# A gated recurrence and a two-layer tanh-shrink network on one core: a shorter polynomial, no elementwise work on GpSimd, the mask on ScalarE, and contiguous token slots

## The chip, the cores and the metric

The kernel runs on one core of a Trainium2 chip. The metric is the device time of one execution in microseconds (us). Engine names in the profile: PE is TensorE's matmul side, PEld its weight loads, DVE is VectorE, ACT is ScalarE, POOL is GpSimd, SP issues the transfers. "L262" is line 262 of the kernel that the profile belongs to; lines move by a few between kernels. "Records" are matmuls as the profile lists them: it has two records for each float32 matmul of the two layers and one for each transpose. "STT" in the prediction is a scalar_tensor_tensor operation of DVE, which takes two tensors and a scalar.

## The reference

```python
# x, f_logit: (4, 6080, 256) float32; lower_bound: (256,)
f = lower_bound + (1 - lower_bound) * sigmoid(f_logit)
h = 0
for t in range(S):                    # along the sequence, for each channel
    h = f[:, t] * h + (1 - f[:, t]) * x[:, t]
    y[:, t] = h
# moe_w_in: (256, 2048), moe_w_out: (2048, 256), float64
h = y.reshape(B * S, D) @ w_in        # 24320 tokens
g = h - tanh(h)
out = g @ w_out
```

The difference `h - tanh(h)` loses its digits where h is small, so both kernels compute it a second way, with a polynomial in h squared, and choose element by element.

## The kernel before

Tokens go through in 47 blocks of 512 and one of 256. A block has 8 slots. In each slot TensorE computes two chunks of 128 rows of h (4 matmuls of 512 columns, 8 records, hT) and, for the block before, 8 matmuls of the second layer (256 columns, 16 records, psO). Between these, four slots carry the pieces of the next block's recurrence (transposes, sigmoid, f, v, scan). The first block also turns the eight weight pieces from float64 bits into float32 on DVE.

The elementwise part of a slot, on tiles of 128 partitions by 1024:

```python
nc.scalar.copy(out=hs, in_=hT[:, :, 0:nb])
nc.scalar.activation(out=t, in_=hT[:, :, 0:nb], func=AF.Square)
nc.scalar.activation(out=th, in_=hT[:, :, 0:nb], func=AF.Tanh)
for n, (a, _, _) in enumerate(QUADS):                      # two quadratics in t
    nc.scalar.activation(out=sq[n], in_=t, func=AF.Square, scale=a, bias=...)
nc.vector.tensor_scalar(out=mask, in0=t, scalar1=SMALL, scalar2=None, op0=ALU.is_lt)
nc.gpsimd.tensor_tensor(out=g, in0=hs, in1=th, op=ALU.subtract)
nc.gpsimd.tensor_tensor(out=hs, in0=hs, in1=t, op=ALU.mult)
for n, (_, _, c) in enumerate(QUADS):
    nc.vector.scalar_tensor_tensor(out=hs, in0=sq[n], scalar=c, in1=hs, op0=ALU.add, op1=ALU.mult)
nc.vector.copy_predicated(out=g, mask=mask, data=hs)
```

The second layer reads its weights (the stationary operand) from g with a step of `ns` = 4 tokens, and inputs and outputs lie in memory so that one partition holds four tokens in a row:

```python
lhsT=gs[j, fc // 2][:, fc % 2, i:nb:ns]                    # second_layer
in_=srcs[s][t0 : t0 + nb, :].rearrange("(p i) d -> p i d", p=P)   # fetch
```

The next block but one is fetched at the end of a block: a store and two loads stand behind each other in one queue.

## Time and profile before

| | before |
|---|---|
| median (lowest to highest; a fourth run came later, with the result) | 3606.25 us (3606.09 to 3609.78, 3 runs) |
| span of the profiled execution | 3607.2 us |
| one block, store to store | 73.3 us |
| busy: DVE, TensorE, ACT, GpSimd | 96%, 84%, 55%, 61% of the span |

The shares are quoted in the prediction, with the rows of the operations. Two more views belong to the argument. The first is the chain of work that ended last, by engine, as the page of the kernel before has it: the shares say on which engine the end depended for how long.

```profile
DVE 60%; issue 24%; ACT 8%; POOL 4%; PE 3%; DMA 1%; DVEq 0%; SPq 0%; ACTq 0%; POOLq 0%
```

The second is the table of waits of the kernel before: engine, tile and line, whom it waited for, us in all, times, the longest.

```profile
ACT hs L249 <- DVE gT L265: 1439.8, 353, 10.6
...
PE tT L173 <- DMA fn<-in_f_logit_dram: 250.3, 46, 6.6
```

ACT, far from busy, is held back by DVE in nearly every slot. TensorE's longest wait comes once a block, for the transfer of f_logit, while DVE goes on working: that wait cost nothing.

### The profile page before, as it was taken

How to read it: one execution, taken by the hardware profiler on the slowest of the kernel's cores; microseconds unless marked ns; L12 is line 12 of the kernel's file. 1: busy time of each engine (PE TensorE's matmuls, PEld its weight loads, DVE VectorE, ACT ScalarE, POOL GpSimd, SP SyncE). 2: the span in 40 equal slices, each digit the busy share in tenths (PEclk: the TensorE clock that was granted, in tenths of full speed). 3: DMA queues.
4: the chain of work that ended last, by engine and by line, in shares of the span. 5: the costliest groups of instructions: out<-in, count | busy, mean ns of one | idle time of the engine just before them, and what ended most of it. 6: DMA issues, size and time to landing. Idle time of an engine off the chain costs nothing.

```text
span 3607.2 us, 27433 instructions
## 1 busy us (share of the span) xinstructions
PE 3021.7 (84%) x9912; PEld 2187.5 (61%) x9912; DVE 3448.1 (96%) x1898; ACT 1970.7 (55%) x2207; POOL 2186.1 (61%) x774
## 2 busy tenths in 40 slices
PE   2388888888888888888888888888888888888888
PEld 1166656666666656666666656665666666665667
DVE  6699999999999999999999999999999999999996
ACT  2255555555555555555555555555555555555554
POOL 2256666666666666666666666666666666666664
PEclk7699999999999989999999999999999999999999
DMA  2100000000100010000000010001000000001000
GB/s 93 35 18 18 18 30 23 18 18 18 35 18 18 18 35 18 18 18 25 28 18 18 18 35 18 18 18 35 18 18 18 21 32 18 18 18 35 18 12 15
DMA packets 24344, 84.87 MB, mean 24 GB/s; under 512 B 2704, under 2 KB 2704, under 8 KB 24208
## 3 DMA queue, kind: packets, MB, share of 16 engines
q1 hardware_dynamic: 24208, 83.11, 6.7%
q8 instruction: 79, 1.29, 0.2%
q14 instruction: 57, 0.47, 0.0%
HBM read 58.20 MB, written 24.90 MB: 23 GB/s over the span
## 4 chain that ended last, share of the span: by engine, by line
DVE 60%; issue 24%; ACT 8%; POOL 4%; PE 3%; DMA 1%; DVEq 0%; SPq 0%; ACTq 0%; POOLq 0%
DVE hs L262 25%; DVE gT L265 16%; DVE mask L256 10%; DVE f L197 6%; ACT s L253 2%; ACT hs L249 2%; POOL hs L260 2%; ACT t L250 2%; POOL gT L259 2%; DVE v L201 2%; PE psO L281 2%; PE hT L234 1%; ACT th L251 1%; DVE y L213 1%; DMA fn<-in_f_logit_dram 0%
## 5 line engine op out<-in xcount | busy, mean ns | idle before, releaser
L259 POOL TENSOR_TENSOR gT<-hs,th 128x1024 f32<-128x1024 f32 (+1 forms) x384 | 967.8, 2520 | 1373.9 <-ACT th L251 1263.5
L234 PE MATMUL hT<-y,w_in 128*128 128x512 f32 (+1 forms) x3072 | 1532.4, 647 | 197.0 <-DVE w_in L148 105.4
L281 PEld LDWEIGHTS psO<-w_out,gT 128*128 128x128 f32 x6080 | 1474.3, 326 | 160.7 <-issue 87.6
L281 PE MATMUL psO<-w_out,gT 128*128 128x256 f32 x6080 | 1476.5, 396 | 24.8 <-DVE w_out L148 15.3
L249 ACT COPY hs<-hT 128x1024 f32<-128x1024 f32 (+1 forms) x384 | 385.4, 1004 | 1611.8 <-DVE gT L265 1439.8
L260 POOL TENSOR_TENSOR hs<-hs,t 128x1024 f32<-128x1024 f32 (+1 forms) x384 | 1217.6, 3171 | 30.1
L262 DVE SCALAR_TENSOR_TENSOR hs<-s,hs 128x1024 f32<-128x1024 f32 (+1 forms) x768 | 1131.0, 1473 | 78.6 <-POOL hs L260 37.1
L234 PEld LDWEIGHTS hT<-y,w_in 128*128 128x128 f32 x3072 | 634.1, 214 | 858.0 <-issue 736.3
L265 DVE COPY_PREDICATED gT<-mask,hs 128x1024 f32<-128x1024 uint8 (+1 forms) x384 | 1081.8, 2817 | 20.3 <-PE hT L234 0.5
L253 ACT ACTIVATE s<-t,shift 128x1024 f32<-128x1024 f32 (+1 forms) x768 | 836.6, 1150 | 0.0
L256 DVE TENSOR_SCALAR mask<-t 128x1024 uint8<-128x1024 f32 (+1 forms) x384 | 640.0, 1667 | 33.9 <-ACT t L250 33.9
L251 ACT ACTIVATE th<-hT 128x1024 f32<-128x1024 f32 (+1 forms) x384 | 393.1, 1024 | 0.0
L250 ACT ACTIVATE t<-hT 128x1024 f32<-128x1024 f32 (+1 forms) x384 | 392.4, 1022 | 0.0
L213 DVE TENSOR_TENSOR_SCAN y<-f,y,v 128x512 f32<-128x512 f32 (+4 forms) x94 | 297.0, 3160 | 3.4
L173 PE MATMUL tT<-ident,fn 128*128 128x128 f32 x380 | 79.2, 345 | 250.3 <-DMA fn<-in_f_logit_dram 250.3
L197 DVE TENSOR_SCALAR f<-u,nom 128x512 f32<-128x512 f32 (+1 forms) x96 | 238.0, 2480 | 0.1
L173 PEld LDWEIGHTS tT<-ident,fn 128*128 128x128 f32 x380 | 57.3, 177 | 268.3 <-DMA fn<-in_f_logit_dram 259.4
L173 PE MATMUL tT<-ident,xn 128*128 128x128 f32 x380 | 67.9, 307 | 110.1 <-DVE v L201 108.9
L173 PEld LDWEIGHTS tT<-ident,xn 128*128 128x128 f32 x380 | 49.7, 157 | 129.0 <-DVE v L201 122.3
L289 ACT COPY osb<-psO 128x256 f32<-128x256 f32 x190 | 71.9, 378 | 15.9 <-PE psO L281 15.9
L201 DVE SCALAR_TENSOR_TENSOR v<-u,om,tT 128x512 f32<-128x512 f32 (+1 forms) x96 | 70.0, 729 | 0.0
L185 ACT ACTIVATE u<-tT 128x512 f32<-128x512 f32 (+1 forms) x96 | 57.5, 599 | 5.1 <-PE tT L173 5.1
(21 smaller groups left out, 81.3 us busy)
## 6 DMA issues: line engine op xcount, KB each, us to landing
fn<-in_f_logit_dram SPq DMA_DIRECT2D x47, 512.0 KB, 4.1
xn<-in_x_dram SPq DMA_DIRECT2D x47, 512.0 KB, 5.1
out_dram<-osb SPq DMA_DIRECT2D x47, 512.0 KB, 2.9
raw<-in_moe_w_in_dram SPq DMA_DIRECT2D x4, 1024.0 KB, 6.5
raw<-in_moe_w_out_dram SPq DMA_DIRECT2D x4, 1024.0 KB, 5.1
fn<-in_f_logit_dram SPq DMA_DIRECT2D x1, 256.0 KB, 3.2
xn<-in_x_dram SPq DMA_DIRECT2D x1, 256.0 KB, 3.4
out_dram<-osb SPq DMA_DIRECT2D x1, 256.0 KB, 2.0
```

What stands on the lines that cost most here:

```text
L197: nc.vector.tensor_scalar(out=f[:, 0:nb], in0=u[:, 0:nb], scalar1=nom[:, h : h + 1], scalar2=1.0, op0=ALU.mult, op1=ALU.add,)
L234: nc.tensor.matmul(hT[:, c, 0:nb], lhsT=w_in_cols(2 * p + c, k), rhs=ys[j][:, k, 0:nb], start=(k == 0), stop=(k == KC - 1),)
L249: nc.scalar.copy(out=hs, in_=hT[:, :, 0:nb])
L250: nc.scalar.activation(out=t, in_=hT[:, :, 0:nb], func=AF.Square)
L251: nc.scalar.activation(out=th, in_=hT[:, :, 0:nb], func=AF.Tanh)
L253: nc.scalar.activation(out=sq[n], in_=t, func=AF.Square, scale=a, bias=shift[:, n : n + 1])
L256: nc.vector.tensor_scalar(out=mask, in0=t, scalar1=SMALL, scalar2=None, op0=ALU.is_lt)
L259: nc.gpsimd.tensor_tensor(out=g, in0=hs, in1=th, op=ALU.subtract)
L260: nc.gpsimd.tensor_tensor(out=hs, in0=hs, in1=t, op=ALU.mult)
L262: nc.vector.scalar_tensor_tensor(out=hs, in0=sq[n], scalar=c, in1=hs, op0=ALU.add, op1=ALU.mult)
L265: nc.vector.copy_predicated(out=g, mask=mask, data=hs)
L281: nc.tensor.matmul(ps[:], lhsT=gs[j, fc // 2][:, fc % 2, i:nb:ns], rhs=w_out_rows(fc), start=(fc == 0), stop=(fc == FC - 1),)
```

## The change

The intent is to take GpSimd out of the way of DVE, to shorten the elementwise work, and to speed up the weight loads. Where h squared is below 0.16 the value is tanh(h) times h squared times one quadratic in h squared. The slot then has four passes on ACT and four on DVE, none on GpSimd; the subtraction reads h straight from PSUM; the predicated copy of one slot is issued in the middle of the next. Besides, f_logit and x are transposed together into one PSUM tile, that pool has three tiles, and all weight loads are issued at the start. The scratch tiles have three buffers instead of two. The core of the diff (cut; deleted comments, renamed tiles, buffer counts in SBUF and the joined transposes are left out):

```diff
-SMALL = 0.35
-QUADS = (...)
+SMALL = 0.16
+QA, QB, QC = -0.045459185935280914, 0.24438677692776334, 0.2736084102289697
 ...
-    ps_t = ctx.enter_context(tc.tile_pool(name="ps_t", bufs=2, space=PSUM))
-    ps_h = ctx.enter_context(tc.tile_pool(name="ps_h", bufs=2, space=PSUM))
+    ps_h = ctx.enter_context(tc.tile_pool(name="ps_h", bufs=3, space=PSUM))
 ...
-                in_=srcs[s][t0 : t0 + nb, :].rearrange("(p i) d -> p i d", p=P),
+                in_=srcs[s][t0 : t0 + nb, :].rearrange("(i p) d -> p i d", p=P),
 ...
+        nc.scalar.activation(out=t, in_=h, func=AF.Square)
+        nc.scalar.activation(out=th, in_=h, func=AF.Tanh)
+        nc.scalar.activation(out=sq, in_=t, func=AF.Square, scale=QA, bias=bias[:, 0:1])
+        nc.scalar.activation(
+            out=small, in_=t, func=AF.Relu, scale=-1.0, bias=bias[:, 1:2]
+        )
+        nc.vector.tensor_tensor(out=g, in0=h, in1=th, op=ALU.subtract)
+        nc.vector.scalar_tensor_tensor(
+            out=sq, in0=sq, scalar=QC, in1=th, op0=ALU.add, op1=ALU.mult
+        )
+        choose()
+        nc.vector.tensor_tensor(out=sq, in0=sq, in1=t, op=ALU.mult)
+        late.append((g, small.bitcast(INT32), sq))
+
+    def choose():
+        if late:
+            g, mask, q = late.pop()
+            nc.vector.copy_predicated(out=g, mask=mask, data=q)
 ...
-                lhsT=gs[j, fc // 2][:, fc % 2, i:nb:ns],
+                lhsT=gs[j, fc // 4][:, fc % 4, i * P : (i + 1) * P],
 ...
-        for n in order[:3]:
+        for n in order:
             fetch_weight(n)
```

More of the change, by code (lines that the diff above doesn't have):

```diff
@@ L15 @@
 P = 128
-SMALL = 0.35
-QUADS = (
-    (0.2820323407649994, 0.18348582088947296, 0.5017573237419128),
-    (0.2820323407649994, -0.6548143625259399, 0.1937771886587143),
-)
+SMALL = 0.16
+QA, QB, QC = -0.045459185935280914, 0.24438677692776334, 0.2736084102289697
 @with_exitstack
@@ L69 @@
     const = ctx.enter_context(tc.tile_pool(name="const", bufs=1))
-    rawpool = ctx.enter_context(tc.tile_pool(name="raw", bufs=3))
     natpool = ctx.enter_context(tc.tile_pool(name="nat", bufs=2))
@@ L73 @@
     ypool = ctx.enter_context(tc.tile_pool(name="ypool", bufs=2))
-    tpool = ctx.enter_context(tc.tile_pool(name="tpool", bufs=2))
-    gpool = ctx.enter_context(tc.tile_pool(name="gpool", bufs=2 * NP))
+    tpool = ctx.enter_context(tc.tile_pool(name="tpool", bufs=3))
+    gpool = ctx.enter_context(tc.tile_pool(name="gpool", bufs=NP))
     opool = ctx.enter_context(tc.tile_pool(name="opool", bufs=2))
-    ps_t = ctx.enter_context(tc.tile_pool(name="ps_t", bufs=2, space=PSUM))
-    ps_h = ctx.enter_context(tc.tile_pool(name="ps_h", bufs=2, space=PSUM))
+    ps_h = ctx.enter_context(tc.tile_pool(name="ps_h", bufs=3, space=PSUM))
     ps_o = ctx.enter_context(tc.tile_pool(name="ps_o", bufs=2, space=PSUM))
@@ L84 @@
     nom = const.tile([P, KC], FP32, name="nom")
-    shift = const.tile([P, 2], FP32, name="shift")
+    bias = const.tile([P, 2], FP32, name="bias")
     w_in = [const.tile([P, KC * TB], FP32, name=f"w_in{g}") for g in range(NG)]
@@ L101, in fetch_weight @@
         g = n % NG
-        raw = rawpool.tile([P, KC * TB], mybir.dt.int64, name="raw")
+        raw = gpool.tile([P, KC * TB], mybir.dt.int64, name="raw", tag="gT")
         if n < NG:
@@ L119, in round_weight @@
         dst = weights[n][:]
-        e = tpool.tile([P, KC * TB], INT32, name="e", tag="hs")
+        e = tpool.tile([P, KC * TB], INT32, name="e", tag="sq")
         m = tpool.tile([P, KC * TB], INT32, name="m", tag="t")
@@ L166 @@
     us = {}
-    def turn(j, s, h):
-        ns = sizes[j] // P
-        dst = ps_t.tile([P, NQ, P], FP32, name="tT")
-        for i in range(ns):
-            nc.tensor.transpose(
-                dst[:, i, :], nats[j, s][:, i, h * P : (h + 1) * P], ident[:]
-            )
-        return dst[:, 0:ns, :].rearrange("p i m -> p m i")
-    def by_slot(t, nb):
-        return t[:, 0:nb].rearrange("p (m i) -> p m i", m=P)
     def gate(j, h):
         nb = sizes[j]
-        fT = turn(j, 0, h)
+        both = ps_h.tile([P, 2, TB], FP32, name="fx", tag="hT")
+        for s in range(2):
+            for i in range(nb // P):
+                nc.tensor.transpose(
+                    both[:, s, i * P : (i + 1) * P],
+                    nats[j, s][:, i, h * P : (h + 1) * P],
+                    ident[:],
+                )
         u = midpool.tile([P, TB], FP32, name="u")
-        nc.scalar.activation(out=by_slot(u, nb), in_=fT, func=AF.Sigmoid, scale=-1.0)
-        us[j, h] = u
+        nc.scalar.activation(
+            out=u[:, 0:nb], in_=both[:, 0, 0:nb], func=AF.Sigmoid, scale=-1.0
+        )
+        us[j, h] = (u, both)
     def recur(j, h):
@@ L192, in recur @@
             ys[j] = ypool.tile([P, KC, TB], FP32, name="y")
-        y, u = ys[j], us.pop((j, h))
-        xT = turn(j, 1, h)
+        y = ys[j]
+        u, both = us.pop((j, h))
         f = midpool.tile([P, TB], FP32, name="f")
         v = midpool.tile([P, TB], FP32, name="v")
+        nc.vector.scalar_tensor_tensor(
+            out=v[:, 0:nb], in0=u[:, 0:nb], scalar=om[:, h : h + 1],
+            in1=both[:, 1, 0:nb], op0=ALU.mult, op1=ALU.mult,
+        )
         nc.vector.tensor_scalar(
@@ L199, in recur @@
             op0=ALU.mult, op1=ALU.add,
-        )
-        nc.vector.scalar_tensor_tensor(
-            out=by_slot(v, nb), in0=by_slot(u, nb), scalar=om[:, h : h + 1], in1=xT,
-            op0=ALU.mult, op1=ALU.mult,
         )
@@ L224 @@
     gs = {}
+    late = []
     def first_layer(j, p):
         nb = sizes[j]
-        hT = ps_h.tile([P, 2, TB], FP32, name="hT")
+        hT = ps_h.tile([P, 2, TB], FP32, name="hT", tag="hT")
         for c in range(2):
@@ L240, in first_layer @@
                 )
-        def temp(tag, dtype=FP32):
-            return tpool.tile([P, 2, TB], dtype, name=tag, tag=tag)[:, :, 0:nb]
-        hs, t, th, mask = temp("hs"), temp("t"), temp("th"), temp("mask", UINT8)
-        sq = [temp("s0"), temp("s1")]
-        gT = gpool.tile([P, 2, TB], FP32, name="gT")
-        g = gT[:, :, 0:nb]
-        nc.scalar.copy(out=hs, in_=hT[:, :, 0:nb])
-        nc.scalar.activation(out=t, in_=hT[:, :, 0:nb], func=AF.Square)
-        nc.scalar.activation(out=th, in_=hT[:, :, 0:nb], func=AF.Tanh)
@@ L252, in first_layer @@
-        for n, (a, _, _) in enumerate(QUADS):
-            nc.scalar.activation(
-                out=sq[n], in_=t, func=AF.Square, scale=a, bias=shift[:, n : n + 1]
-            )
-        nc.vector.tensor_scalar(
-            out=mask, in0=t, scalar1=SMALL, scalar2=None, op0=ALU.is_lt
-        )
-        nc.gpsimd.tensor_tensor(out=g, in0=hs, in1=th, op=ALU.subtract)
-        nc.gpsimd.tensor_tensor(out=hs, in0=hs, in1=t, op=ALU.mult)
-        for n, (_, _, c) in enumerate(QUADS):
-            nc.vector.scalar_tensor_tensor(
-                out=hs, in0=sq[n], scalar=c, in1=hs, op0=ALU.add, op1=ALU.mult
-            )
@@ L265, in first_layer, with temp @@
-        nc.vector.copy_predicated(out=g, mask=mask, data=hs)
-        gs[j, p] = gT
+        h = hT[:, :, 0:nb]
+        def temp(tag):
+            return tpool.tile([P, 2, TB], FP32, name=tag, tag=tag)[:, :, 0:nb]
+        t, th, sq, small = temp("t"), temp("th"), temp("sq"), temp("small")
+        if p % 2 == 0:
+            gs[j, p // 2] = gpool.tile([P, 4, TB], FP32, name="gT", tag="gT")
+        c0 = 2 * (p % 2)
+        g = gs[j, p // 2][:, c0 : c0 + 2, 0:nb]
+        nc.scalar.activation(out=t, in_=h, func=AF.Square)
@@ new lines, in first_layer @@
+        nc.scalar.activation(out=th, in_=h, func=AF.Tanh)
+        nc.scalar.activation(out=sq, in_=t, func=AF.Square, scale=QA, bias=bias[:, 0:1])
+        nc.scalar.activation(
+            out=small, in_=t, func=AF.Relu, scale=-1.0, bias=bias[:, 1:2]
+        )
+        nc.vector.tensor_tensor(out=g, in0=h, in1=th, op=ALU.subtract)
+        nc.vector.scalar_tensor_tensor(
+            out=sq, in0=sq, scalar=QC, in1=th, op0=ALU.add, op1=ALU.mult
+        )
+        choose()
+        nc.vector.tensor_tensor(out=sq, in0=sq, in1=t, op=ALU.mult)
@@ L291, in second_layer @@
                     nc.sync.dma_start(
-                        out=out[t0 : t0 + nb, :].rearrange("(p i) d -> p i d", p=P),
+                        out=out[t0 : t0 + nb, :].rearrange("(i p) d -> p i d", p=P),
                         in_=osb[:, 0:ns, :],
@@ L303 @@
         nc.sync.dma_start(out=lb[:], in_=lower_bound.rearrange("(h p) -> p h", p=P))
-        for n in order[:3]:
+        for n in order:
             fetch_weight(n)
         fetch(1)
-        for n, (_, b, _) in enumerate(QUADS):
-            nc.vector.memset(shift[:, n : n + 1], b)
+        nc.vector.memset(bias[:, 0:1], QB)
+        nc.vector.memset(bias[:, 1:2], SMALL)
         nc.vector.tensor_scalar(
@@ L321 @@
                     first_layer(j, p)
+                elif p == 0:
+                    choose()
                 if j > 0:
@@ L327 @@
                     round_weight(order[p])
-                if j == 0 and 3 + p < 2 * NG:
-                    fetch_weight(order[3 + p])
             if j + 2 < NBLK:
```

## The prediction

> **What bounds the kernel now.** I read the page's busy shares and slices first. Columns: engine, busy us and share of the span, instructions; then one digit (tenths busy) per fortieth of the span.
>
> ```profile
> PE 3021.7 (84%) x9912; PEld 2187.5 (61%) x9912; DVE 3448.1 (96%) x1898; ACT 1970.7 (55%) x2207; POOL 2186.1 (61%) x774
> DVE  6699999999999999999999999999999999999996
> PEclk7699999999999989999999999999999999999999
> ```
>
> DVE is full in every slice after the start; nothing else is. The chain that ended last agrees: DVE 60%, ACT 8%, POOL 4%, PE 3%. Next, the groups with shapes kept apart: count, busy us, mean ns of one.
>
> ```profile
> L260 POOL TENSOR_TENSOR hs<-hs,t 128x1024 f32<-128x1024 f32 x376 | 1206.2, 3208 | 29.5
> L262 DVE SCALAR_TENSOR_TENSOR hs<-s,hs 128x1024 f32<-128x1024 f32 x752 | 1119.9, 1489 | 63.2 <-POOL hs L260 22.6 <-ACT t L250 0.9 <-ACT s L253 0.9
> L265 DVE COPY_PREDICATED gT<-mask,hs 128x1024 f32<-128x1024 uint8 x376 | 1074.8, 2858 | 19.4 <-PE hT L234 0.5
> L256 DVE TENSOR_SCALAR mask<-t 128x1024 uint8<-128x1024 f32 x376 | 634.6, 1688 | 33.9 <-ACT t L250 33.9
> L197 DVE TENSOR_SCALAR f<-u,nom 128x512 f32<-128x512 f32 x94 | 233.2, 2481 | 0.1
> ```
>
> These means are not the cost of the work but of work beside GpSimd. The timeline of the start, where GpSimd happens to be idle, has the same operations alone (start us, duration us):
>
> ```profile
> 7.68 0.48 DVE L197 TENSOR_SCALAR f<-u,nom 128x512 f32<-128x512 f32 x1
> 8.85 1.22 DVE L213 TENSOR_TENSOR_SCAN y<-f,v 128x512 f32<-128x512 f32 x1
> 18.17 1.23 DVE L148 SCALAR_TENSOR_TENSOR w_in<-w_in,e 128x1024 f32<-128x1024 f32 x1
> 44.78 1.29 DVE L265 COPY_PREDICATED gT<-mask,hs 128x1024 f32<-128x1024 uint8 x1
> ```
>
> So f costs 0.48 us alone and 2.48 in the stream, the scan 1.22 against 3.22, the predicated copy 1.29 against 2.86, the mask 0.69 against 1.69. That is the bound: DVE does much of its time waiting inside its instructions. One block of 512 tokens takes 73.3 us (store to store, 243.59 to 316.86), and there are 47.5 blocks.
>
> The second engine is TensorE. From the timeline and the view of one line in two windows (3400 to 3500 us, whole blocks; then 3590 to the end, the half block):
>
> ```profile
> 1578.08 3.60 PE L234 MATMUL hT<-y,w_in 128*128 128x512 f32 x8
> 1581.51 3.88 PE L281 MATMUL psO<-w_out,gT 128*128 128x256 f32 x16
> L281 PEld LDWEIGHTS psO<-w_out,gT x176: 308/329/333, 3408.4 to 3498.1; 128*128 128x128 f32 x176
> ...
> 3589.17 14.68 PE L281 MATMUL psO<-w_out,gT 128*128 128x256 f32 x67
> ...
> L281 PEld LDWEIGHTS psO<-w_out,gT x63: 195/197/198, 3589.9 to 3603.3; 128*128 128x128 f32 x63
> ```
>
> Start to start, an hT matmul record takes (3.60 - 0.59) / 7 = 0.430 us, a psO record (3.88 - 0.40) / 15 = 0.232. In the half block, where the weights are read with a step of 2 floats and not 4, a weight load takes 197 ns instead of 329, and the psO record only (14.68 - 0.38) / 66 = 0.217. In whole blocks the weight load sets the pace.
>
> **What the Trainium skill says.** (1) "SBUF — State Buffer", Who interferes with whom: a DVE instruction with two SBUF inputs, or in a two-port mode, contends with a GpSimd instruction that reads SBUF, and the later one blocks. The trace agrees (0.48 against 2.48 us). (2) "Advanced Engine Details and Errata", SBUF Cachelines: lines of 16 bytes, at least two hits on one are needed. The trace agrees: a step of 16 bytes 329 ns, of 8 bytes 197. (3) "TensorE: Matmul & The Clock Gate", Part 1: after an idle window of some 3.4 us the clock halves, and it needs about as long to come back. The trace agrees: in the windows view, TensorE idle from 1562.6 to 1568.4 us is followed by a granted clock of 0.53 until 1571.8 and then 1.00. (4) "VectorE: DVE Perf Modes", TRN2 errata: a PSUM source costs 120 cycles fixed against 58 from SBUF. Here v, half in PSUM, takes 0.734 us for 512 elements, 0.20 over 512/0.96; I use that for the new subtraction.
>
> **The change, part by part, for a whole block** (8 slots of two d_ff chunks).
>
> GpSimd: both elementwise passes go (2.5 + 3.2 us a slot), so nothing locks DVE's port any more.
>
> DVE: of mask, two STT and predicated copy there stay one STT (1.23) and the copy (1.29); new are h - tanh from PSUM (1024/0.96 + 0.20 = 1.27) and a tensor by tensor product (like an STT, 1.23). 5.0 us a slot, 40 a block. The recurrence is 2 x (0.74 + 0.48 + 1.22) = 4.9. DVE: 45 us a block.
>
> ACT: copy out of PSUM goes, the second square becomes the Relu that makes the mask: five passes become four. From their starts in the timeline (0.92 to 1.05 us apart) 4.0 a slot, 32 a block, and 4 x 0.38 + 2 x 0.60 = 2.7: 35 us.
>
> TensorE: 64 hT records x 0.430 = 27.5; 128 psO records x 0.217 = 27.7, because token slots are now contiguous in the weights and the load drops to 197 ns or below; 16 transposes x 0.11 (four in 0.60 with a tail of some 0.27) = 1.75. Sum 56.9 us a block if never idle. This is the largest of the four engines, so TensorE becomes the bound. Nothing of the smaller terms lies on the path as long as buffers hold.
>
> Do they hold? PSUM has three tiles for hT and the joined f/x transposes, the old pair of transposes is gone. An hT tile is free when tanh and the subtraction have run: some 2.0 + 1.3 us after its last matmul, and it is wanted again two slots (some 13 us) later. Slots 1 and 3 carry 5.0 + 2.4 us on DVE against 6.9 on TensorE, less than a slot of lag, made up in the next. The predicated copy comes one slot late; the last of a block is finished some 2 us into slot 1 of the next and is needed near that slot's end. No wait seen there.
>
> DMA: a store and two loads follow each other at the end of every block. Today TensorE waits 259 us in all for f_logit (45 waits, about 5.8 each), since the store, ahead in the same queue, waits for ACT, which lags behind DVE. After the change ACT keeps up: the last output copy ends about 1 us after TensorE's last matmul of the block (ACT still owes 0.7 us of the slot's passes, then 0.38), the store issues at +1.1, f_logit at +1.5, x at +2.0. With today's landings (4.1 and 5.1 us) they are there at +5.6 and +7.1. TensorE asks for f_logit at 27.5/8 + 27.7/8 = +6.9, for x at +7.3. The rows in memory go from 4 KB to 1 KB, which may add some 0.5 us: packets of 4096 and 2048 bytes took 159 and 84 ns, so by a straight line 1024 bytes take 47, 16% less throughput. I put 0.3 us of wait on a block; far under the idle time that halves the clock. 57.2 us a block.
>
> Start: before, the second store (end of the second pass) was issued at 243.6. There the four stages of weight rounding took some 42 us each. Rounding one weight stays 7.15 us (12.29 to 19.45); the stage becomes two of these, a cold first hT and two ACT passes (about 7.5), two DVE slots of 5, and 2.4 for a scan in the first two: 34 us. All weight loads are now issued ahead of the second block's inputs, about 8.4 MB at near 400 GB/s, so those land near 31 us and delay the second slot by perhaps 6 us. Walking it through gives hT of the last stage at 127, the last rounding done at 152, the end of the second pass at 199: 45 us saved.
>
> End: half block of first layer with a whole block of second 13.8 + 27.7 = 41.5, last second layer 13.8, copy and store 3.
>
> Sum: 199 + 45 x 57.2 + 41.5 + 13.8 + 3 = 2831; some semaphore time on top, 2838 us.
>
> **Rivals.** (a) The input wait moves onto the new bound: if landings slip 2 us more than I reckon (1 KB rows, three transfers at once), every block pays 2: 2925. For it: margin is only 0.2 us, and x is now needed together with f_logit, two slots earlier than x was. Against: packets at 2 KB showed no loss worth 1 us. (b) DVE stays the bound: it would need 57 us a block, a quarter more than the sum of its parts; only if the slowdown had another source than GpSimd. The half-empty start speaks against it. With the old durations it would be 3600. (c) The psO pace stays at 0.232, because N = 256 and not the load limits it: 2 us a block, 2930. The half block at 0.217 is against. (d) Continuous matmuls draw a lower clock: at 13/16, the figure that the same TensorE page gives for three busy cores of a die, 70 us a block, 3400. In this trace the windows without idle TensorE show 1.00 over 16 us (1574 to 1590), so unlikely.
>
> **Range and chances.** No wait at all and a shorter start give 2800; (a) or (c) in part give 2920. Every rival but (b) and (d) is well over 2% faster: faster 0.98, same 0.015, slower 0.005.
>
> **What would show it.** In the new profile: no POOL work in the stream, PE near 97% and DVE near 77% busy; stores 57 us apart; the scan near 1.2 us, predicated copy near 1.3; weight loads for psO at 197 ns or under and psO records 0.217 apart; granted clock near 1.0; waits of TensorE for fn and xn some tens of us in sum. It is wrong if DVE instructions stay stretched, if fn or xn waits exceed 1 us a block, or if the clock falls under load.

## The result, and the profile after

| | before | after |
|---|---|---|
| median (lowest to highest) | 3607.03 us (3606.09 to 3609.78, 4 runs) | 2827.36 us (2826.4 to 2828.49, 4 runs) |
| ratio, with its 95% interval | 1 | 0.7838 (0.7827 to 0.7849) |
| one block, store to store | 73.3 us | 57.08 us (mean) |
| first store issued at (end of the second pass) | 243.6 us | 200.5 us |

The change took 21.6% off the time. 45 blocks at 73.3 - 57.08 = 16.2 us are 730 us of the 780, the start is 43 us, the end some 7. (The prediction and some expectations call the store at the end of the second pass "the second store"; the queue shows none before it, so it is the first.)

The page after, first its busy shares, then three of the rows of forty slices (tenths busy; for PEclk the granted clock in tenths), then the chain that ended last by engine and by line:

```profile
PE 2726.5 (96%) x9912; PEld 1823.7 (65%) x9912; DVE 2065.9 (73%) x1898; ACT 1635.0 (58%) x1823; POOL 0.7 (0%) x6
...
PE   3399999999999999999999999999999999999999
...
DVE  5777777777777777777777777777777777777774
...
PEclk6699999999999999999999999999999999999999
...
PE 89%; DMA 4%; DVE 3%; ACT 2%; issue 1%; SPq 1%; ACTq 0%
PE hT L228 44%; PE psO L277 42%; DMA xn<-in_x_dram 4%; PE fx L171 3%; ACT th L246 1%; ACT sq L247 1%; SPq L155 0%; SPq L105 0%; DVE gT L251 0%; DVE sq L252 0%; DVE e L130 0%; ACT small L248 0%; DVE sq L256 0%; ACT osb L285 0%; SPq L287 0%
```

The full row of nines has moved from DVE to PE, and with it the chain: from DVE 60% to PE 89%. DVE has a quarter of its time free. From 500 to 2500 us the windows view has PE busy for 1998 us of 2000, DVE for 1483, ACT for 1204, at a granted clock of 1.00; in a block of 57.08 us that is 42.3 us of DVE and 34.4 of ACT. The first two slices (the start, with the rounding of the weights) are all that is left of an idle TensorE.

The groups after, shapes kept apart (count, busy us, mean ns of one, idle time before):

```profile
L277 PEld LDWEIGHTS psO<-w_out,gT 128*128 128x128 f32 x6080 | 1155.8, 190 | 319.2 <-issue 176.0 <-DVE w_out L144 2.6 <-DVE gT L262 2.4
...
L262 DVE COPY_PREDICATED gT<-small,sq 128x1024 f32<-128x1024 int32 x376 | 508.0, 1351 | 0.0
L256 DVE TENSOR_TENSOR sq<-sq,t 128x1024 f32<-128x1024 f32 x376 | 460.7, 1225 | 0.0
L251 DVE TENSOR_TENSOR gT<-hT,th 128x1024 f32<-128x1024 f32 x376 | 458.4, 1219 | 714.4 <-ACT th L246 714.4
L252 DVE SCALAR_TENSOR_TENSOR sq<-sq,th 128x1024 f32<-128x1024 f32 x376 | 456.9, 1215 | 0.0
L207 DVE TENSOR_TENSOR_SCAN y<-f,y,v 128x512 f32<-128x512 f32 x86 | 110.4, 1284 | 3.0
...
L195 DVE TENSOR_SCALAR f<-u,nom 128x512 f32<-128x512 f32 x94 | 46.7, 497 | 0.0
```

Nothing is stretched any more: the predicated copy fell from 2858 to 1351 ns, f from 2481 to 497, the scan from 3224 to 1284. DVE's idle time (714 us) is spent waiting for tanh at the start of a slot, which in turn waits for TensorE. The psO weight load has a mean of 190 ns, against 326 before.

What is left of idle TensorE inside the stream shows in the table of waits after:

```profile
PEld fx L171 <- DMA xn<-in_x_dram: 12.4, 35, 0.8
...
PE fx L171 <- DMA fn<-in_f_logit_dram: 8.4, 2, 4.9
...
PE fx L171 <- DMA xn<-in_x_dram: 3.4, 12, 0.6
```

The 250 us for f_logit are gone; x is now the input that comes last, by tenths of a microsecond a block (the two waits for f_logit are at the start). Where this comes from is in the timeline of one block's end after (start us, duration us, engine, line):

```profile
1513.78 3.60 PE L228 MATMUL hT<-y,w_in 128*128 128x512 f32 x8
...
1514.43 0.37 ACT L285 COPY osb<-psO 128x256 f32<-128x256 f32 x1
...
1514.82 0.38 SPq L287 DMA_DIRECT2D out_dram<-osb  x1
...
1515.30 0.46 SPq L155 DMA_DIRECT2D fn<-in_f_logit_dram  x1
...
1515.86 0.74 SPq L155 DMA_DIRECT2D xn<-in_x_dram  x1
...
1517.21 3.62 PE L277 MATMUL psO<-w_out,gT 128*128 128x256 f32 x16
...
1520.66 0.60 PE L171 MATMUL fx<-ident,fn 128*128 128x128 f32 x4
...
1521.26 0.66 PE L171 MATMUL fx<-ident,xn 128*128 128x128 f32 x4
```

ACT's last copy of the old block, then the store, then the two loads follow each other; x is asked for at 1521.1 and there at 1521.26, so the two groups of transposes are 0.60 us apart, where they are 0.44 apart without a wait (the second pair of groups in each block). The psO records are (3.62 - 0.38) / 15 = 0.216 us apart, the hT records 0.430 as before.

### The profile page after: what moved, and what is told of

Read it like the earlier page. It is cut to its first block, busy times and chain, and to the rows that moved or that the text cites. A ratio compares the mean times of both kernels' runs of the same rounds, so it can differ in the third digit from the quotient of the medians.

```text
span 2826.7 us, 25181 instructions
## 1 busy us (share of the span) xinstructions
PE 2726.5 (96%) x9912; PEld 1823.7 (65%) x9912; DVE 2065.9 (73%) x1898; ACT 1635.0 (58%) x1823; POOL 0.7 (0%) x6
## 3 DMA queue, kind: packets, MB, share of 16 engines
q8 instruction: 78, 1.28, 0.2%
## 4 chain that ended last, share of the span: by engine, by line
PE 89%; DMA 4%; DVE 3%; ACT 2%; issue 1%; SPq 1%; ACTq 0%
PE hT L228 44%; PE psO L277 42%; DMA xn<-in_x_dram 4%; PE fx L171 3%; ACT th L246 1%; ACT sq L247 1%; SPq L155 0%; SPq L105 0%; DVE gT L251 0%; DVE sq L252 0%; DVE e L130 0%; ACT small L248 0%; DVE sq L256 0%; ACT osb L285 0%; SPq L287 0%
## 5 line engine op out<-in xcount | busy, mean ns | idle before, releaser
L228 PE MATMUL hT<-y,w_in 128*128 128x512 f32 (+1 forms) x3072 | 1380.2, 592 | 80.2 <-DVE w_in L144 80.2
L277 PEld LDWEIGHTS psO<-w_out,gT 128*128 128x128 f32 x6080 | 1155.8, 190 | 319.2 <-issue 176.0
L251 DVE TENSOR_TENSOR gT<-hT,th 128x1024 f32<-128x1024 f32 (+1 forms) x384 | 463.9, 1208 | 732.1 <-ACT th L246 732.1
L262 DVE COPY_PREDICATED gT<-small,sq 128x1024 f32<-128x1024 int32 (+1 forms) x384 | 513.8, 1338 | 0.1
L256 DVE TENSOR_TENSOR sq<-sq,t 128x1024 f32<-128x1024 f32 (+1 forms) x384 | 466.1, 1214 | 0.0
L252 DVE SCALAR_TENSOR_TENSOR sq<-sq,th 128x1024 f32<-128x1024 f32 (+1 forms) x384 | 462.5, 1204 | 0.0
L247 ACT ACTIVATE sq<-t,bias 128x1024 f32<-128x1024 f32 (+1 forms) x384 | 438.0, 1141 | 2.6 <-DVE w_out L144 2.0
L248 ACT ACTIVATE small<-t,bias 128x1024 f32<-128x1024 f32 (+1 forms) x384 | 437.5, 1139 | 0.0
L207 DVE TENSOR_TENSOR_SCAN y<-f,y,v 128x512 f32<-128x512 f32 (+4 forms) x94 | 118.0, 1255 | 3.3
L177 ACT ACTIVATE u<-fx 128x512 f32<-128x512 f32 (+1 forms) x96 | 56.9, 593 | 47.1 <-PE fx L171 47.1
L171 PE MATMUL fx<-ident,xn 128*128 128x128 f32 x380 | 60.4, 282 | 4.2 <-DMA xn<-in_x_dram 3.4
L195 DVE TENSOR_SCALAR f<-u,nom 128x512 f32<-128x512 f32 (+1 forms) x96 | 47.4, 494 | 0.0
L130 DVE SCALAR_TENSOR_TENSOR e<-raw,e 128x1024 int32<-128x1024 int32 x8 | 9.8, 1225 | 0.3
```

The source lines that it names most:

```text
L171: nc.tensor.transpose(both[:, s, i * P : (i + 1) * P], nats[j, s][:, i, h * P : (h + 1) * P], ident[:],)
L207: nc.vector.tensor_tensor_scan(out=y[:, h, a:e], data0=f[:, a:e], data1=v[:, a:e], initial=init, op0=ALU.mult, op1=ALU.add,)
L228: nc.tensor.matmul(hT[:, c, 0:nb], lhsT=w_in_cols(2 * p + c, k), rhs=ys[j][:, k, 0:nb], start=(k == 0), stop=(k == KC - 1),)
L247: nc.scalar.activation(out=sq, in_=t, func=AF.Square, scale=QA, bias=bias[:, 0:1])
L248: nc.scalar.activation(out=small, in_=t, func=AF.Relu, scale=-1.0, bias=bias[:, 1:2])
L251: nc.vector.tensor_tensor(out=g, in0=h, in1=th, op=ALU.subtract)
```

## The experiments

The theory: GpSimd's two passes locked DVE's second port and so stretched every DVE instruction that needs it; without them DVE falls below TensorE, and TensorE at its own pace (weight loads at step 1) sets the block, with a small wait for the input at each block's end. The rivals: it is the shorter polynomial that does it and GpSimd was harmless; or it is the layout; or the chain's share for x is worth what it says. Twelve kernels ran, all with a correct result; those called b_ are edits of the kernel before, those called a_ edits of the kernel after. The diffs are cut; ` ...` stands for what is left out.

| run | edit | median us | ratio to before (95%) |
|---|---|---|---|
| b_no_gps | before, the two GpSimd passes on DVE | 3000.83 | 0.8318 (0.8305 to 0.833) |
| b_layout | before, contiguous slots | 3600.33 | 0.9977 (0.9963 to 0.9992) |
| b_no_gps_layout | both | 2997.65 | 0.8305 (0.8292 to 0.8319) |
| a_gps_work | after, two passes on GpSimd | 2884.04 | 0.7993 (0.798 to 0.8007) |
| a_gps_dummy | after, two passes on GpSimd added that nobody reads | 3434.74 | 0.9516 (0.9502 to 0.953) |
| a_gps_memset | after, four memsets on GpSimd added | 2863.1 | 0.7938 (0.7925 to 0.7952) |
| a_gps_memset_early | the same with earlier loads | 2823.24 | 0.7823 (0.7812 to 0.7835) |
| a_stride | after, weights read at step 4 | 2915.6 | 0.8082 (0.8071 to 0.8093) |
| a_mask_dve | after, mask on DVE | 2819.75 | 0.7817 (0.7806 to 0.7827) |
| a_psum2 | after, two PSUM tiles for hT | 2844.45 | 0.7886 (0.7874 to 0.7897) |
| a_early | after, loads issued in slot 4 | 2817.82 | 0.7809 (0.7798 to 0.7819) |
| a_best | the same with another start | 2778.15 | 0.77 (0.7689 to 0.7711) |

### b_no_gps: the old arithmetic, all of it on DVE

```diff
-        nc.gpsimd.tensor_tensor(out=g, in0=hs, in1=th, op=ALU.subtract)
-        nc.gpsimd.tensor_tensor(out=hs, in0=hs, in1=t, op=ALU.mult)
+        nc.vector.tensor_tensor(out=g, in0=hs, in1=th, op=ALU.subtract)
+        nc.vector.tensor_tensor(out=hs, in0=hs, in1=t, op=ALU.mult)
```

> The kernel before with its two GpSimd passes moved to the Vector engine, nothing else. Theory (the Vector engine's time in the kernel before is its own work plus the time it stands still while GpSimd holds the shared port): a slot costs mask 0.69 + five two-input passes of about 1.15 to 1.25 = 6.8 us, a block 54 to 56 + 4.9 = 59 to 61 us, about what TensorE needs with the strided weights (64 x 0.430 + 128 x 0.232 + 1.75 = 59), so some 2950 to 3100 us in all. Rival (the Vector engine is simply overloaded and GpSimd takes work off it): two more passes at the stretched 1.5 to 2.8 us make a block 95 us or more, over 4300 us.

Measured: 3000.83 us, in the theory's range and far from the rival's 4300. DVE was given two more passes a slot, and the time fell by 17%. The groups of this run:

```profile
L262 DVE SCALAR_TENSOR_TENSOR hs<-s,hs 128x1024 f32<-128x1024 f32 x752 | 921.4, 1225 | 80.8 <-DVE hs L262 1.4 <-DVE hs L260 0.9 <-ACT t L250 0.5
...
L265 DVE COPY_PREDICATED gT<-mask,hs 128x1024 f32<-128x1024 uint8 x376 | 495.0, 1317 | 12.9
...
L256 DVE TENSOR_SCALAR mask<-t 128x1024 uint8<-128x1024 f32 x376 | 254.9, 678 | 31.3 <-ACT t L250 31.3
```

The predicated copy is at 1317 ns, the passes of L262 at 1225, the mask at 678, the scan at 1284: all back at about what they cost alone. A block is 60.5 us, and the first store goes out at 214.5 us, so 29 of the 43 us that the start gained are here too. So most of the gain is to be had without the new polynomial, by moving work onto the busiest engine.

### a_gps_dummy: GpSimd passes that nobody reads

```diff
+        spare = temp("spare")
+        for _ in range(2):
+            nc.gpsimd.tensor_tensor(out=spare, in0=t, in1=th, op=ALU.subtract)
         nc.vector.tensor_tensor(out=sq, in0=sq, in1=t, op=ALU.mult)
```

> The changed kernel with two added GpSimd subtractions of 128 x 1024 in each slot, whose result nobody reads; they only wait for tanh. Theory of the exclusive port: the Vector engine's two-input passes are held up by the 4.7 us of GpSimd a slot: 3.5 + 4.7 = 8.2 us a slot at least, 66 + 3.4 = 69 us a block, up to 79 when the subtraction from PSUM doesn't overlap either; so 3350 to 3850 us. Rival (the stretched durations of the kernel before were waits for GpSimd's results): nobody waits for these, so 2827 us within 1% and passes at 1.2 us.

Measured: 3434.74 us; the theory holds. Nobody reads the result of these passes (ACT waited seven times for them to be done with a buffer, 14.5 us in all), and they cost 607 us; from 1000 to 2000 us DVE is busy for 999. The groups of this run:

```profile
L258 POOL TENSOR_TENSOR spare<-t,th 128x1024 f32<-128x1024 f32 x752 | 2347.0, 3124 | 1017.8 <-ACT th L246 986.6
...
L265 DVE COPY_PREDICATED gT<-small,sq 128x1024 f32<-128x1024 int32 x376 | 1021.2, 2716 | 0.0
L252 DVE SCALAR_TENSOR_TENSOR sq<-sq,th 128x1024 f32<-128x1024 f32 x376 | 829.4, 2206 | 0.0
...
L259 DVE TENSOR_TENSOR sq<-sq,t 128x1024 f32<-128x1024 f32 x376 | 562.7, 1496 | 0.0
L251 DVE TENSOR_TENSOR gT<-hT,th 128x1024 f32<-128x1024 f32 x376 | 456.3, 1214 | 39.8 <-ACT th L246 39.8
```

The predicated copy and L252 have two SBUF inputs and are stretched to 2716 and 2206 ns. The last product (L259) has two as well and is stretched less, to 1496; why it meets GpSimd less was not traced. The subtraction has one input in PSUM: it stays at 1214. The block, 69.6 us, fits the same picture by an estimate: DVE's own 42.3 us and 16 GpSimd passes of some 2.35 us (their duration when they need not wait, from the start of the timeline before) are 79.9; if the passes with a PSUM input run beside GpSimd, 8 x 1.14 + 2 x 0.66 = 10.4 comes off (their durations less the 0.1 us by which passes overlap), which leaves 69.5.

### a_gps_work: the new arithmetic with GpSimd doing part of it

```diff
+        hs = temp("hs")
+        nc.scalar.copy(out=hs, in_=h)
 ...
-        nc.vector.tensor_tensor(out=g, in0=h, in1=th, op=ALU.subtract)
+        nc.gpsimd.tensor_tensor(out=g, in0=hs, in1=th, op=ALU.subtract)
 ...
-        nc.vector.tensor_tensor(out=sq, in0=sq, in1=t, op=ALU.mult)
+        nc.gpsimd.tensor_tensor(out=sq, in0=sq, in1=t, op=ALU.mult)
```

> The changed kernel with h - tanh(h) and the last product given back to GpSimd (and the copy of h out of PSUM that GpSimd needs). Theory of the exclusive port: in each slot GpSimd needs the port for 2 x 2.35 us and the Vector engine for 2.4 (one two-input product, one predicated copy), 7.1 in sum, x 8 = 57, and 3.4 for f and the scan: 60 to 62 us a block against 57, so 2950 to 3080 us, and the Vector engine's predicated copy stretched from 1.35 to over 2 us. Rival (only the amount of work counts): the Vector engine has two passes fewer, TensorE stays the bound, 2827 us within 1%.

Measured: 2884.04 us, 2% over the kernel after: neither range. The lock is there (predicated copy 2434 ns, L254 1754, scan 3223, f 1904), but it does not decide. DVE has only two of its own passes left in the slot, and with the stretch it is busy 763 us in 1000, so TensorE still sets the block, at 57.9 us. Of the 57 us more, some 16 lie in the start (first store at 216.5 and not 200.5). Most of the rest is the wait for x: the two first groups of transposes of a block are on average 1.24 us apart and not 0.60. ACT has five passes again, its last copy ends 1.82 us after the block's last matmul and not 0.86, and so store and loads start later. The expectation added durations up as if each held the port throughout. By that sum, 7.1 x 8 + 3.4 = 60.2 us, DVE would have been the bound: it is too long.

### b_layout: contiguous slots alone

```diff
-                in_=srcs[s][t0 : t0 + nb, :].rearrange("(p i) d -> p i d", p=P),
+                in_=srcs[s][t0 : t0 + nb, :].rearrange("(i p) d -> p i d", p=P),
 ...
-                lhsT=gs[j, fc // 2][:, fc % 2, i:nb:ns],
+                lhsT=gs[j, fc // 2][:, fc % 2, i * P : (i + 1) * P],
 ...
```

> The kernel before with only the token slots made contiguous (loads, store, weights of the second layer, the recurrence's views). Theory: weight loads for the second layer go from 329 to about 190 ns and the matmul records from 0.233 to 0.216 us apart, which takes 2 us a block off TensorE, but TensorE isn't the bound there, so the time stays within 1% of 3607 us. Rival (TensorE and the Vector engine share the path): up to 2.1 us x 47 = 100 us less, 3510 us.

Measured: 3600.33 us, 0.2% faster. The weight load is 190 ns and the psO spacing 0.216 us, just as after, and it is worth next to nothing while DVE is the bound.

### a_stride: the new kernel with the old step

```diff
-                lhsT=gs[j, fc // 4][:, fc % 4, i * P : (i + 1) * P],
+                lhsT=gs[j, fc // 4][:, fc % 4, i:nb:ns],
 ...
-                        out=out[t0 : t0 + nb, :].rearrange("(i p) d -> p i d", p=P),
+                        out=out[t0 : t0 + nb, :].rearrange("(p i) d -> p i d", p=P),
```

> The changed kernel with only the weights of the second layer read with a step of 4 floats again (and the store by partition to match, so the result stays right). Theory (the weight load sets the pace of the second layer's records): loads 329 ns for 190, records 0.233 apart for 0.2155, on 6016 records of the whole blocks 0.0172 x 6016 = 103 us: 2930 us, 59.2 us a block. Rival (the step only mattered beside the other engines' traffic, or the pace comes from N = 256): 2827 us within 0.5%.

Measured: 2915.6 us. The same edit that was worth 7 us before is worth 88 here. The row of the weight loads in the groups of this run:

```profile
L277 PEld LDWEIGHTS psO<-w_out,gT 128*128 128x128 f32 x6080 | 1473.5, 325 | 138.1 <-issue 88.0 <-DVE w_out L144 2.1 <-DVE gT L262 2.1
```

The spacing of psO is 0.233 us and not 0.216: for 6080 records, 103 us. The run has 88. Some 6 us of the difference are the wait for x, which all but vanishes with a slower TensorE (the two groups of transposes that come first in a block are on average 0.47 us apart from 500 to 2500 us, and 0.60 after); the rest was not traced. So the prediction's rival (c), a pace that N = 256 sets, is out.

### a_mask_dve: the mask made on DVE

```diff
 ...
-        nc.scalar.activation(
-            out=small, in_=t, func=AF.Relu, scale=-1.0, bias=bias[:, 1:2]
-        )
+        nc.vector.tensor_scalar(
+            out=small, in0=t, scalar1=SMALL, scalar2=None, op0=ALU.is_lt
+        )
 ...
```

> The changed kernel with the mask made by the Vector engine again (a compare to bytes instead of the Relu on ScalarE). Theory: the Vector engine gets 0.6 us a slot more, 42 to 47 us of a 57 us block, still hidden; 2827 us within 0.3%, so this part of the change is worth nothing once TensorE is the bound. Rival (the Vector engine is near enough to the bound that slots 1 and 3, 5.2 + 2.4 us against 6.9, push TensorE): 1 to 2% slower.

Measured: 2819.75 us (2818.31 to 2822.67). The theory's range holds, and the median is even 7.6 us lower than after. DVE is busy 82% instead of 73 and ACT 45% instead of 58, and neither matters by itself. But ACT's last copy of a block now ends 0.41 us after the last matmul and not 0.86, x lands 6.9 us after it and not 7.3, and TensorE hardly waits: a block is 56.85 us for 57.08, 10 us over 45 blocks, of which the start loses 4 (first store at 204.3 us). This part of the change costs a little; the intervals of the two ratios just touch, but the blocks in the traces say the same.

### a_early: the loads a block ahead

```diff
                 if p < len(steps):
                     steps[p]()
+                if p == 4 and j + 2 < NBLK:
+                    fetch(j + 2)
 ...
-            if j + 2 < NBLK:
-                fetch(j + 2)
```

> The changed kernel with the loads of the next inputs issued in the middle of a block (slot 4) rather than after the store at its end. Two readings of the profile of the changed kernel compete. The chain that ended last puts 4% of the span (113 us) on the load of x: by it, 2715 us. TensorE's own idle time before the transposes is 12 us, and the transposes' spacing shows perhaps 10 to 14 us lost in all (20.6 us for 96 steps that take 0.109 when nothing waits): by it, 2813 to 2818 us. I expect the second.

In the queue the loads of a block now stand ahead of the store of the same pass and not behind it: in this run's timeline a fourth pair of loads goes out at 68 us, before the first store, where the kernel after has three. From there on a pair still goes out right behind a store (201.7 us behind 201.2), but it is needed a block later.

Measured: 2817.82 us (2815.39 to 2818.02). The chain's "DMA 4%" is 113 us, TensorE's idle time for x about a tenth of that; the run gave 9.5 us. The chain puts all the time of a transfer down to it once that transfer came last, also the part in which TensorE worked. The timeline of this run's PE:

```profile
1514.52 0.60 PE L171 MATMUL fx<-ident,fn 128*128 128x128 f32 x4
1514.96 0.60 PE L171 MATMUL fx<-ident,xn 128*128 128x128 f32 x4
1515.40 3.60 PE L228 MATMUL hT<-y,w_in 128*128 128x512 f32 x8
```

The groups are 0.44 us apart, and a block is 56.8 us, the 56.9 of the prediction's sum for a TensorE that never idles.

### a_best: the same, with the weights rounded in another order

```diff
-    order = [n for g in range(NG) for n in (g, NG + g)]
+    order = list(range(2 * NG))
+    before_slot = {0: (0, 1, 2)}
+    after_slot = {3: (3,), 5: (4,), 6: (5,), 7: (6, 7)}
 ...
-                if j == 0 and p % 2 == 0:
-                    round_weight(order[p])
+                if j == 0:
+                    for n in before_slot.get(p, ()):
+                        round_weight(n)
 ...
-                if j == 0 and p % 2 == 1:
-                    round_weight(order[p])
 ...
+                if j == 0 and p in after_slot:
+                    if p == 7:
+                        choose()
+                    for n in after_slot[p]:
+                        round_weight(n)
```

The first block has no second layer beside it, so the pieces of w_in are rounded first and those of w_out, which the second block needs, as late as they can be (with the edit of a_early too).

> The early loads, and the start put in another order: three of the four parts of w_in rounded before the first slot, the fourth after slot 3, and w_out rounded after slots 5 to 7, so that the Vector engine doesn't stand still four times (8.4, 7.5, 8.7, 8.5 and 7.9 us in the changed kernel) for a cold first-layer matmul. Theory (the start is bound by the Vector engine's 57 us of rounding and 41 us of slots and scans, and the waits between them come on top): the second pass ends some 40 us earlier, 2815 - 40 = 2775 us. Rival (TensorE's cold clock or the order of the weight loads sets the start): 2805 to 2815 us.

Measured: 2778.15 us (2777.22 to 2779.19, 5 runs). The first store goes out at 162.4 us and not at 201.2 as in a_early, and these 38.8 us are nearly the whole gain over it (39.7). It is the fastest of all, 1.7% faster than the kernel after.

### a_psum2: two tiles for hT instead of three

```diff
-    ps_h = ctx.enter_context(tc.tile_pool(name="ps_h", bufs=3, space=PSUM))
+    ps_h = ctx.enter_context(tc.tile_pool(name="ps_h", bufs=2, space=PSUM))
```

> The changed kernel with two PSUM tiles for the first layer and the transposes instead of three. Theory (the third tile is what lets the joined f and x transposes sit in the same pool): the matmuls of slots 2 and 4 wait until v has read the transposes, each time some 3.9 us a block beyond TensorE's natural start, and an idle time of that length also halves its clock for a while: 7.7 us a block more at least, 3180 to 3400 us. Rival (ACT and the Vector engine free tiles fast enough with two): 2827 us within 1%.

Measured: 2844.45 us, 17 more than after. My theory's range was missed by 336 us, and the rival's 1% holds. The step that failed: it assumed that two tiles are used in turn, so that an hT of the second slot has to wait until v has read the transposes in the other tile. The timeline says otherwise:

```profile
1537.49 1.23 DVE L251 TENSOR_TENSOR gT<-hT,th 128x1024 f32<-128x1024 f32 x1 [3.31 <-ACT th L246]
...
1538.77 0.30 PEld L228 LDWEIGHTS hT<-y,w_in 128*128 128x128 f32 x2 [0.24 <-DVE gT L251]
1538.77 3.70 PE L228 MATMUL hT<-y,w_in 128*128 128x512 f32 x8
...
1542.14 0.73 DVE L191 SCALAR_TENSOR_TENSOR v<-u,om,fx 128x512 f32<-128x512 f32 x1
```

The matmul starts as soon as the subtraction has read the other hT tile (1537.49 + 1.23 = 1538.72), long before v. So it did not have to wait for the transposes' tile, and what it waits for comes just in time: the cost is about 0.1 us in such slots (a block is 57.28 us for 57.08) and one wait of 8.3 us at 153 us, in the start.

### a_gps_memset and a_gps_memset_early: a busy GpSimd that does not read

```diff
+    tick = const.tile([P, 2], FP32, name="tick")
 ...
+        spare = temp("spare")
+        for _ in range(4):
+            nc.gpsimd.memset(spare, 0.0)
+        nc.scalar.copy(out=tick[:], in_=spare[:, 0, 0:2])
```

The small copy on ACT (128 x 2) keeps GpSimd in step.

> The changed kernel with four added GpSimd memsets of 128 x 1024 in each slot, which only write; ScalarE reads two columns of the result so that they keep pace. Theory (the Vector engine's two-input passes contend with GpSimd's reads only): the two-input passes stay at 1.2 us, only f, the one pass in a two-port mode, may stretch from 0.5 us, and the time stays at 2827 us within 1%. Rival (any GpSimd access holds the port): like the two subtractions, over 3200 us if a memset takes 1 us or more.

Measured: 2863.1 us, 36 more than after: neither the 2827 nor the rival's 3200. The groups of this run:

```profile
L259 POOL MEMSET spare<- 128x1024 f32 x1504 | 1433.0, 953 | 1352.9 <-ACT tick L260 1288.2
...
L253 DVE SCALAR_TENSOR_TENSOR sq<-sq,th 128x1024 f32<-128x1024 f32 x376 | 456.9, 1215 | 0.0
...
L196 DVE TENSOR_SCALAR f<-u,nom 128x512 f32<-128x512 f32 x94 | 103.9, 1105 | 0.0
```

GpSimd is busy half of the time, and the passes with two SBUF inputs stay at 1215 ns; only f, with one input, is stretched (0.50 to 1.10 us). A memset reads nothing, a subtraction reads two tensors; so GpSimd's reading is what stretches the former, as far as a memset stands for all passes that only write. The 36 us lie elsewhere (29 in the blocks, 6 in the start): the loads land 5.0 and 5.9 us after their issue (4.5 and 5.3 after), x takes 1.00 us to issue and not 0.74, and TensorE waits for x some 0.8 us a block. To test that, the same memsets with the loads of a_early:

> The changed kernel with the four GpSimd memsets a slot and the early loads together. The memsets alone cost 36 us while the Vector engine's two-input passes stayed at 1.22 us; x landed 0.6 us later after its issue and TensorE waited for it at every block. Theory (the memsets cost only through that wait): with the loads early nothing is left of it, 2818 us as with the early loads alone, within 0.3%. Rival (the memsets hold up the Vector engine after all, f at 1.1 us for 0.5): some 2 x 0.6 us a block, up to 2870 us.

Measured: 2823.24 us, 0.2% over a_early, with blocks of 56.8 us as there. In the stream the memsets cost only through the input wait; the 5 us that are left lie in the start (first store at 206.6 us and not 201.2). Why transfers land later beside them was not isolated: the extra ACT pass and the memsets came together.

### b_no_gps_layout: GpSimd and layout undone together

The edits of b_no_gps and of b_layout, on the kernel before.

> The kernel before with both its GpSimd passes on the Vector engine and the contiguous token slots, that is, the change without the new polynomial and without the new buffers. Alone the layout gave 0.2% and the move off GpSimd 17%. Theory (after the move two engines are near the bound, TensorE 59.0 and the Vector engine 58.2 of a 60.5 us block): TensorE falls to 56.9 and the Vector engine alone sets the pace, 58.5 to 59.5 us a block, 2910 to 2955 us; the rest to 2827 is the polynomial's shorter work on the Vector engine. Rival (the layout is worth its full 2.1 us a block as soon as GpSimd is idle): 2905 us or less.

Measured: 2997.65 us: both missed. The layout is worth 3 us here too, and a block is still 60.4 us. I had taken DVE's need from its busy time, 58.2 us a block, and expected that to set the pace. The timeline of DVE in this run:

```profile
1511.71 0.67 DVE L256 TENSOR_SCALAR mask<-t 128x1024 uint8<-128x1024 f32 x1
1512.30 1.22 DVE L259 TENSOR_TENSOR gT<-hs,th 128x1024 f32<-128x1024 f32 x1
1513.55 1.23 DVE L260 TENSOR_TENSOR hs<-hs,t 128x1024 f32<-128x1024 f32 x1
1514.88 2.56 DVE L262 SCALAR_TENSOR_TENSOR hs<-s,hs 128x1024 f32<-128x1024 f32 x2
1517.47 1.30 DVE L265 COPY_PREDICATED gT<-mask,hs 128x1024 f32<-128x1024 uint8 x1
1518.67 0.68 DVE L256 TENSOR_SCALAR mask<-t 128x1024 uint8<-128x1024 f32 x1
```

L262 reads what L260 wrote, and starts 1.33 us after it, 0.10 after its end. A slot is 1518.67 - 1511.71 = 6.96 us; eight of them and two stretches of v, f and scan at 2.37 us are 60.4. So DVE is the bound with no idle time that one could see in its share. The same view of the kernel after:

```profile
1505.61 1.23 DVE L251 TENSOR_TENSOR gT<-hT,th 128x1024 f32<-128x1024 f32 x1 [2.15 <-ACT th L246]
1506.75 1.22 DVE L252 SCALAR_TENSOR_TENSOR sq<-sq,th 128x1024 f32<-128x1024 f32 x1
1507.88 1.34 DVE L262 COPY_PREDICATED gT<-small,sq 128x1024 f32<-128x1024 int32 x1
1509.12 1.20 DVE L256 TENSOR_TENSOR sq<-sq,t 128x1024 f32<-128x1024 f32 x1
```

Here each pass starts 0.09 to 0.10 us before the one ahead of it has ended. No pass here reads what the one just ahead writes, or overwrites what it reads, since the copy of the slot before stands between L252 and L256. The kernel after has one pair that does depend: the scan reads f from just ahead, and starts after its end (f at 8.56 us for 0.48, the scan at 9.08). That dependence is the cause is read from such pairs; no run changed the order alone.

## Why the prediction was right

The time came out at 2827.4 us where 2838 was predicted. By its steps:

- **GpSimd's lock.** Right, and shown by three runs from both sides: taking it away alone (b_no_gps, -606 us), adding passes that nobody reads (a_gps_dummy, +607 us), and GpSimd work without reads (a_gps_memset, two-input passes unchanged). For f the prediction's sentence was too narrow, since it has f held up by GpSimd's reads alone: beside memsets f went from 0.50 to 1.10 us. The durations came as predicted: 1.28 us for the scan, 1.35 for the predicated copy, 0.50 for f.
- **DVE 45 us a block.** 42.3 measured. The subtraction from PSUM took 1219 ns and not 1270, and passes that do not depend on each other overlap by some 0.1 us. So the term for PSUM that the prediction took over from v was too large here, and DVE was busy 73% and not 77. It was not on the path either way.
- **ACT 35 us a block.** 34.4 measured. The prediction left ACT off the path, "as long as buffers hold". That is right for its sum, but not for the last passes of a block, which stand ahead of the store and the loads: a_mask_dve takes one ACT pass away and gains 7.6 us, and a_gps_work adds one and waits longer for x.
- **TensorE 56.9 us a block and the new bound.** Right; a_early, with no input wait left, has 56.8. The psO spacing is 0.216 and the weight load 190 ns, as predicted; a_stride puts a price of 88 us on it.
- **Input wait 0.3 us a block.** 57.08 - 56.83 = 0.25 measured, and 9.5 us in all by a_early. Landings of 4.5 and 5.3 us were within what was allowed for the smaller rows. The 0.3 us was put, not worked out: it stood on a margin of 0.2 us, with some 0.5 open in the landings, so that it came so close is in part luck.
- **Buffers.** They held: no wait for hT, gT or sq of any size in the stream. The margin was larger than thought, since even two PSUM tiles cost only 17 us.
- **Start and end.** The first store was predicted at 199 and came at 200.5; hT of the last stage at 127 (126.7), the last rounding at 152 (150.9). What follows the last whole block's store takes 2826.7 - (200.5 + 45 x 57.08) = 57.6 us, where 41.5 + 13.8 + 3 = 58.3 was summed up.
- **The rest.** The sum was 2831, and 7 us were put on top for semaphores. They are not there: the blocks' mean has them already. This is most of the 10 us by which the number is high.

Of the rivals, (b) and (d) are refuted by the profile after (DVE 73% busy; clock 1.00 in the windows) and (c) by its psO spacing of 0.216 us and by a_stride. Rival (a), the input wait, is there at a tenth of its size.

How the 780 us divide depends on the order, because two bounds lie close together. From before: no GpSimd work -606, then contiguous slots -3, then the rest of the change (shorter polynomial, late copy, buffers, start) -170; these last were not taken apart. From after, four parts undone, each alone: GpSimd work +57, step of four +88, two PSUM tiles +17, mask on DVE -8. With the new arithmetic two passes on GpSimd in place of DVE cost 57 us where they cost 606 with the old, since DVE, with only two passes of its own left, then has room. Open are two sizes. Durations summed as port time come out some 4% too long: before, 16 x 2.35 + 8 x (0.68 + 2 x 1.22 + 1.29) + 2 x (0.48 + 1.22) = 76.3 for 73.3, and in a_gps_work 60.2, where DVE had room in 57.9. And why the loads land later beside memsets was not isolated.

## What to carry to other kernels

When an engine is full, look for the same instruction in a stretch where the neighbours are idle: if it is shorter there, the engine is waiting inside its instructions, and moving work onto it from the neighbour that holds it up can make it faster. A faster pace on an engine that is not the bound is worth nothing until it is (the weight loads: 7 us, then 88), so price each part against the bound that will hold after the change. A chain's share for a transfer is not what its removal saves; count the idle time of the bound in front of it (113 against 10 us here), and don't read a share of 96% as 4% of room when the passes depend on each other.

## What the Trainium skill lacked or had wrong

- "VectorE: DVE Perf Modes", the TRN2 errata: its table has 120 cycles fixed for a PSUM source and 58 for SBUF, which the prediction used; the page itself says that its VectorE row is too low for single operations. A subtraction with one input in PSUM took 1219 ns, a product from SBUF alone 1225: no difference. The page's other formula, (N + 151)/0.96, gives 1224 ns for 1024 elements and fits both. It doesn't fit v (512 elements, one input in PSUM, a scalar for each partition): 758 ns in the kernel after, where it gives 691; the cause was not isolated.
- The same page, The DRAIN you can't avoid: for eight copies in a row it finds that a semaphore after each costs nothing extra. Here a pass that depends on the one just ahead starts 0.03 to 0.10 us after its end, an independent one 0.08 to 0.12 before it; in b_no_gps_layout that makes 60.4 us a block for 58.2 busy. Whether the semaphore or something else in the dependence costs this was not isolated.
- "TensorE: Matmul & The Clock Gate", LDWEIGHTS: the time is given by the columns alone. For float32 it depends on the step: 190 ns at step 1, 197 at 2, 325 to 329 at 4, and with the last the records are 0.233 us apart and not 0.216.
- "SBUF — State Buffer", Who interferes with whom: "DMA never contends with a compute engine." Beside GpSimd memsets and a small ACT pass the loads landed 0.5 to 0.6 us later (5.0 and 5.9 for 4.5 and 5.3). The cause was not isolated, so this doesn't refute the sentence. What the section says on DVE and GpSimd the runs bear out in kind (two-input passes at 1215 ns beside memsets, up to 2716 beside subtractions); its "for the whole instruction" would make sums of whole durations right, and by the estimates above they come out some 4% too long.
